# Two attention layers and two ReLU layers on one core: the beginning in another order, and exponentials split only while work is overdue

## The chip, the core and the metric

The kernel runs on one NeuronCore of a Trainium2 chip. Its engines work side by side, each through its own queue of instructions: TensorE (PE in the profile, its weight loads PEld), VectorE (DVE), ScalarE (ACT), GpSimd (POOL), and SyncE (SP), which here issues all DMAs. The metric is the device time of one execution in microseconds (us); the median over several runs counts, and lower is better. For this kernel about 0.5% (11 us) is what a measurement can tell from no change.

## The reference

Four layers follow one another on x of 2048 rows by 512 columns, all in float32, each with a layer norm in front and a residual sum behind it; the weights are the same in both rounds.

```python
def _A_ref(x, wq, wk, wv, wo):            # H = 32 heads, Dh = 16, one shared key and value head
    q = (x @ wq).reshape(B, S, H, Dh).transpose(0, 2, 1, 3)
    k = x @ wk
    v = x @ wv
    scores = jnp.einsum("bhqd,bkd->bhqk", q, k) * (Dh ** -0.5)
    p = _softmax(scores, axis=-1)
    o = jnp.einsum("bhqk,bkd->bhqd", p, v)
    return o.transpose(0, 2, 1, 3).reshape(B, S, H * Dh) @ wo

def _B_ref(x, w1, w2):                    # 512 -> 1792 -> 512
    h = jnp.maximum(jnp.einsum("bsd,df->bsf", x, w1), 0)
    return jnp.einsum("bsf,fd->bsd", h, w2)

x = x + _A_ref(_layernorm(x), wq, wk, wv, wo)
x = x + _B_ref(_layernorm(x), w1, w2)
x = x + _A_ref(_layernorm(x), wq, wk, wv, wo)
x = x + _B_ref(_layernorm(x), w1, w2)
```

## The kernel before

**Units, steps, products.** A unit `U` is four heads for a block of 512 queries; there are 32 units in each of the two rounds. Its keys are taken in 16 tiles of 128. One (unit, key tile) pair is a *step*; there are 1024. A step has two score halves (`scores`: eight small matmuls from `fqop` and `fkop` into a PSUM bank `fst`, then one exponential of 128x1024 on ScalarE into `fp`) and one *product* (`values`: 16 small float32 matmuls of `fp` with the values `fva`, summed in the two banks `facc`). The first 16 steps are units 0 to 3 with the first four key tiles each, the next 16 go back through units 3 to 0 with the next four, and so on. When a unit's stretch ends, `keep` empties the two banks on VectorE (or one of them on ScalarE) into `faccs`; the next unit's products wait for that. Four `fp` buffers let the scores run up to four steps ahead of the products.

**Split exponentials.** In `cut_values` an exponential's float32 bits are taken apart: the upper 16 bits are read as bfloat16, and VectorE writes the rest as float16 over the lower 16 bits (`cut`, two subtractions of 128x1024). The product then takes 24 small 16-bit matmuls instead of 16 in float32. A step so treated is called a cut below. Values for it lie in `fvp`, high and low part, which `keep_keys` fills from `fva`.

**Dense work.** Projections, output and ReLU layers are Python generators in `self.gens`; each `yield 1.0` is one unit of TensorE work. The whole program is laid out in straight order when it is built. `timed` decides at each point whether the next thing on TensorE is a score half, a product or a unit of dense work, by an account of its own (`_Account`, `duration`) that adds up durations for each engine, and a beam search over the next 24 moves. Each step adds `rate` (at least 1) to `due`, the work owed; work may be placed once `due` is at least 1 (`LEAST`), and what stands above 11 (`OVER`) is penalised. A cut is decided when the first exponential of a step ends:

```python
            if chance and self.now >= chance[0][0] - LATE:
                e1, e, i = chance.pop()
                if (self.asked and self.gens and not pend and i > j and self.coming > NEAR
                        and self.sim.at["DVE"] <= max(self.now, e1) + LATE):
                    self.cuts.add(i)
```

`self.asked` counts the chains (output, ReLU layer, next projections) that have been started, so there is no cut before the first of them. `HALF` is the time that half a cut is thought to take on VectorE. Functions can also be hung on a product with `at(i, fn)`; `after(i)` calls them once product `i` has been placed, behind the `keep` of a unit that ends there.

**The beginning (`begin`).** Four row tiles of x are loaded, then the key, value and query weights. VectorE makes their layer norm (`stats`, two small operations on GpSimd in between, `apply` to `fxn`), TensorE transposes them in turn (`transposed`), ScalarE copies the high half and VectorE subtracts the low half, into `fxt`. Behind each, six warm matmuls (`warm`, into `facc`) keep TensorE busy. Weights are split in the same way: `prep_wkv` (wk2 high and low), `prep_wq` for query group 0, later 1, later 2 and 3. `late_consts` fills `va[0]` and `vp[0]` on GpSimd and makes further constants. Then come the key block (`key_rows`, `keep_keys`, `key_norm`: the largest key square is turned, reduced to a row `fkr` and sent into the key operand), and the first query group (`first_query`), whose high half goes to the scratch `fqd` in DRAM in two DMAs and whose low half goes in one. `squares` sums the query squares; for groups 0 and 1 its rows `fqr` go straight into the query operands `fqop`. `load_rows` brings units 0 and 1 back from `fqd` in four DMAs. After that group 1 is formed and projected, 16 warm matmuls follow, and the last two query groups are formed. Only then does `timed` take over with the generator `following` in hand: the squares and loads for units 2 and 3, `rows(8)` (row tiles 4 to 7: `stats`, `apply`, `halved` into `fxp`, a transposing DMA each), then the keys of blocks 1 to 3. Tiles 8 to 15 hang on products 1, 3, 7 and 9.

SP's queue is taken in order: a DMA that waits holds back those behind it.

Of the kernel before, what the change touches and what calls it, by code (L numbers as in the profile page):

```python
# [37 lines left out]
LATE, NEAR, HALF = 0.3, 8, 1.22  # L38
# [20 lines left out]
class _Account:  # L59

    def __init__(self, clear=0.0):
        self.at = {"ACT": 0.0, "DVE": 0.0, "POOL": 0.0, "SP": 0.0, "PE": 0.0}
        self.slots, self.turns, self.uses = {}, {}, {}
        self.form, self.boxes = None, {}
# [62 lines left out]
    def run(self, eng, out, ins, cost):  # L127
        start = max(self.at[eng], self.after(eng, ins, False), self.after(eng, [out], True))
        end = self.at[eng] = start + cost
        if eng == "SP":  # L130
            end += LAND + cost_of(out) * SIZE[out.dtype] * count(out) / FLOW
            eng = "DMA"
# [21 lines left out]
def duration(eng, op, out, ins):  # L154
# [12 lines left out]
    if eng == "DVE":  # L167
        if psum or len([a for a in ins if cost_of(a) > 1]) > 1 or op == "bn_stats":
            return 0.15 + n / 960.0
# [10 lines left out]
class _Engine:  # L180
# [4 lines left out]
    def __getattr__(self, op):  # L185
        fn = getattr(self.eng, op)

        def call(*a, **k):
# [3 lines left out]
            if op == "dma_start":  # L192
                self.account.run("SP", out, ins, TURNED if k.get("transpose") else ISSUE)
# [16 lines left out]
class _Engines:  # L210

    def __init__(self, nc, account):
# [4 lines left out]
        self.sync = _Engine(account, nc.sync, "SP")  # L217


class _Net:  # L220
# [185 lines left out]
    def late_consts(self):  # L406
        nc = self.nc
        nc.gpsimd.memset(self.va[0], self.vs / self.os)
        if not self.exact:
            nc.gpsimd.memset(self.vp[0], self.vs / self.os)  # L410
            nc.gpsimd.memset(self.wms, 0.0)
            wv = self.wt("wvc", [P, 4, DH], bufs=1)
            nc.gpsimd.tensor_copy(wv, self.wvraw[:, :, 1, :])
            self.spread(wv.rearrange("p c d -> p (c d)"), 3, 0)
            nc.gpsimd.memset(self.good, 1.0)
            nc.vector.memset(self.sel, 0.0)
            grp = self.ct("grp", [P, 2, 4])
            nc.vector.reduce_sum(grp.rearrange("p s g -> p (s g)"),
                                 self.ident.rearrange("p (g d) -> p g d", d=DH), axis=AX)
            nc.vector.tensor_add(self.sel[:, 0:4], grp[:, 0], grp[:, 1])  # L420
# [8 lines left out]
    def prep_wkv(self, raw, eng=None):  # L429
# [16 lines left out]
        nc.gpsimd.tensor_sub(self.wk2[1], rr, _f(self.wk2[0]))  # L446
        self.wvraw = raw

# [7 lines left out]
    def prep_wq(self, raw, lo=0, hi=4, tmp=None):  # L456

        nc = self.nc
        if tmp is None:
            tmp = self.wt("p", [P, 4, D], bufs=self.np)  # L460
        if hi - lo < 4:
            for g in range(lo, hi):
                t, r = tmp[:, :, g * P:(g + 1) * P], raw[:, :, g * P:(g + 1) * P]
                for pr in range(2):
                    nc.scalar.activation(t.rearrange("p c (q x d) -> p c q x d", q=2, x=4)[:, :, pr],
                                         r.rearrange("p c (x q d) -> p c x q d", x=4, q=2)[:, :, :, pr],
                                         AF.Copy, scale=self.up / self.xs * DH ** -0.5)
            cols = slice(lo * P, hi * P)
            nc.scalar.activation(self.wq2[0][:, :, cols], tmp[:, :, cols], AF.Copy)
            (nc.gpsimd if lo > 1 else nc.vector).tensor_sub(self.wq2[1][:, :, cols], tmp[:, :, cols], self.wq2[0][:, :, cols])  # L470
            return tmp
# [123 lines left out]
    def keep_keys(self, L, b, pv):  # L595
        nc = self.nc
        nc.vector.tensor_copy(self.va[L][:, 4 * b:4 * b + 4, 0:DH], pv[:, :, 48:64])
        if not self.exact:
# [4 lines left out]
            v, vp = self.va[L][:, 4 * b:4 * b + 4, 0:DH], self.vp[L][:, 4 * b:4 * b + 4]  # L603
            nc.vector.tensor_copy(vp[:, :, 0:DH], v)
            nc.vector.tensor_sub(vp[:, :, 32:48], v, vp[:, :, 0:DH])
        if self.exact or b + 1 != self.normed[L]:
            self.have[L] += 1

# [29 lines left out]
    def squares(self, L, b, groups, sq):  # L638
# [10 lines left out]
        qr = self.wt("qr", [P, 2, D], F16, bufs=1)  # L649
        for pr in range(2):  # L650
            rows = slice(0, 32 * n)
# [1206 lines left out]
```

## Time and profile before

| | |
|---|---|
| median of 3 runs | 2245.5 us (2242.57 to 2253.92) |
| the profiled execution | 2249.38 us, span 2247.6 us |
| TensorE busy | 2162.8 us, 96% |
| ScalarE busy | 1980.6 us, 88%; 1949.1 us of it 2048 exponentials |
| VectorE busy | 1231.6 us, 55%; 505.8 us of it 376 halves of split exponentials |
| GpSimd busy | 279.3 us, 12% |
| first exponential | starts at 32.53 us |

Nearly all instructions pass through one helper, so their line is L189 throughout, and they are told apart by the tiles they write and read (with an `f` in front: `fst<-fqop,fkop` are scores). A row of the timeline has the start, the duration, the engine, and behind it in brackets how long the engine had idled and who ended that. Rows of merged instructions have their count behind an x.

### The profile page before, as it was taken

Reading aid. Unit: us, or ns where it says so; the run is one execution under the profiler, and the core shown is the slowest. Engines: PE = TensorE matmul, PEld = TensorE weight load, DVE = VectorE, ACT = ScalarE, POOL = GpSimd, SP = SyncE. Lnnn points to the kernel's source line nnn. Section 1 sums busy time; section 2 is a strip of 40 time slices with the busy share of each in tenths; the row PEclk is TensorE's granted clock in tenths of the full one; section 3 lists DMA queues with packets and bytes.
Section 4 is the critical chain, followed back from the end, with each engine's and each line's share of the span. In section 5 each row is a group of like instructions: output and inputs, shape, how many; then the busy total and the mean of one; then the engine's idle time right before and its main releaser. Section 6 shows DMA issues by size and latency. Waiting matters only on the chain.

```text
span 2247.6 us, 127404 instructions
## 1 busy us (share of the span) xinstructions
PE 2162.8 (96%) x59949; PEld 1266.5 (56%) x59949; DVE 1231.6 (55%) x1961; ACT 1980.6 (88%) x2111; POOL 279.3 (12%) x321
## 2 busy tenths in 40 slices
PE   7999999999999999999999999999999999999988
PEld 3444445556667864665546555456656655665543
DVE  7426635554565555544676676565634554654642
ACT  5899999999989999999988889889999999999810
POOL 6216830001100021000120021100010000100000
PEclk8999999999999999999999999999999999999999
DMA  5235634111332133221252154532124211312122
GB/s 156 72 109 173 200 103 109 59 49 48 84 104 68 46 95 92 69 68 39 82 130 71 38 141 141 142 87 68 40 73 118 68 49 64 100 42 73 52 81 71
DMA packets 182561, 195.08 MB, mean 87 GB/s; under 512 B 79312, under 2 KB 115712, under 8 KB 181768
## 3 DMA queue, kind: packets, MB, share of 16 engines
q1 hardware_dynamic: 182024, 186.83, 28.1%
q8 instruction: 470, 7.70, 1.4%
q14 instruction: 67, 0.55, 0.1%
HBM read 120.16 MB, written 51.87 MB: 77 GB/s over the span
## 4 chain that ended last, share of the span: by engine, by line
PE 78%; ACT 11%; DVE 5%; issue 2%; DMA 2%; POOL 1%; SPq 0%; DVEq 0%; ACTq 0%; POOLq 0%
PE fmisc L189 31%; PE facc L189 31%; PE fst L189 16%; ACT fp L189 11%; DVE fbst L189 1%; DMA frd<-flsum 1%; DMA fqop<-fqd 1%; DVE faccs L189 0%; DVE fxt L189 0%; SPq L189 0%; DVE fxn L189 0%; DVE fp L189 0%; DVE fqr L189 0%; DMA frinv<-frd 0%; POOL fbmv L189 0%
## 5 line engine op out<-in xcount | busy, mean ns | idle before, releaser
L189 ACT ACTIVATE fp<-fst 128x1024 f32<-128x1024 f32 x2048 | 1949.1, 1030 | 140.2 <-PE fst L189 128.4
L189 PE MATMUL fst<-fqop,fkop 64*32 64x512 f16 x16384 | 952.2, 378 | 43.2 <-ACT fp L189 36.5
L189 PE MATMUL facc<-fp,fva 64*32 64x512 f32 x13376 | 937.8, 593 | 3.3 <-issue 2.0
L189 DVE TENSOR_TENSOR fp<-fp 128x1024 f16<-128x1024 f32 x376 | 505.8, 1398 | 257.5 <-ACT fp L189 257.0
L189 PEld LDWEIGHTS <-fkop 64*32 64x32 f16 x16384 | 382.8, 91 | 460.5 <-issue 347.1
L189 PEld LDWEIGHTS facc<-fp,fva 64*32 64x32 f32 x13376 | 296.9, 106 | 100.2 <-issue 26.4
L189 PE MATMUL fmisc<-fw,fhh 64*32 64x512 f16 (+1 forms) x6384 | 314.3, 377 | 5.1 <-DVE fseen L189 3.1
L189 PEld LDWEIGHTS <-fw 64*32 64x32 f16 (+1 forms) x9576 | 201.6, 93 | 132.5 <-issue 41.8
L189 PE MATMUL fmisc<-fxt,fw 64*32 64x512 f16 (+1 forms) x5544 | 241.1, 376 | 2.1 <-DVE fxt L189 0.9
L189 POOL TENSOR_SCALAR fbmv<-fbmv 128x1 f32<-128x1 f32 x64 | 18.0, 281 | 1560.9 <-DVE fbmv L189 1559.8
L189 PE MATMUL fmisc<-fw,fhl 64*32 64x512 f16 (+1 forms) x3192 | 202.3, 378 | 0.0
L189 PEld LDWEIGHTS <-fhh 64*32 64x32 f16 (+1 forms) x6384 | 142.9, 93 | 87.7 <-issue 39.3
L189 PE MATMUL facc<-fp,fvp 64*32 64x512 f16 (+2 forms) x4512 | 178.2, 386 | 1.7 <-issue 1.7
L189 DVE SCALAR_TENSOR_TENSOR fxt<-fmisc,fxt 128x512 f32<-128x512 f32 x156 | 102.6, 684 | 126.2 <-PE fmisc L189 125.9
L189 PE MATMUL fmisc<-fxq,fw 64*32 64x512 f16 x4032 | 150.1, 376 | 3.3 <-issue 3.1
L189 DVE TENSOR_SCALAR fhh<-fmisc 128x512 f16<-128x512 f32 x98 | 67.2, 686 | 124.5 <-PE fmisc L189 124.4
L189 DVE COPY fseen<-fmisc 1x1 f32<-1x1 f32 x266 | 29.1, 141 | 193.1 <-PE fmisc L189 187.8
L189 DVE TENSOR_TENSOR faccs<-faccs,facc 128x512 f32<-128x512 f32 x116 | 79.6, 686 | 66.6 <-PE facc L189 51.8
L189 PEld LDWEIGHTS <-fvp 64*32 64x32 f16 (+1 forms) x4512 | 89.7, 90 | 44.6 <-issue 10.9
L189 PE MATMUL fmisc<-fwo,fot 64*32 64x512 f16 x2688 | 103.8, 378 | 2.3 <-issue 2.2
L189 DVE SCALAR_TENSOR_TENSOR fhl<-fmisc,fhh 128x512 f16<-128x512 f32 x112 | 77.5, 692 | 28.4 <-ACT fhh L189 25.0
L189 PEld LDWEIGHTS <-fhl 64*32 64x32 f16 (+1 forms) x3192 | 72.8, 93 | 28.6 <-issue 3.0
(139 smaller groups left out, 1114.4 us busy)
## 6 DMA issues: line engine op xcount, KB each, us to landing
fw<-fwd SPq DMA_DIRECT2D x224, 256.0 KB
fod<-faccs SPq DMA_DIRECT2D x62, 256.0 KB
fqop<-fqd SPq DMA_DIRECT2D x152, 98.0 KB
fxt<-in_A_x_dram SPq DMA_DIRECT2D x32, 256.0 KB
fqd<-fqh SPq DMA_DIRECT2D x64, 128.0 KB
foraw<-fod SPq DMA_DIRECT2D x31, 256.0 KB
frinv<-frd SPq DMA_DIRECT2D x31, 256.0 KB
faccs<-in_B_w_dram SPq DMA_DIRECT2D x28, 256.0 KB
```

The source lines that it names most:

```text
L189: r = fn(*a, **k)
```

## The change

Six things are changed.

- `begin`: `va[0]` and `vp[0]` are filled by ScalarE (`filled`, two activations) before the first weights are there, not by GpSimd later. The low half of the key weights is subtracted behind the last row tile: GpSimd first copies one element of it. Query group 0 is scaled and formed on ScalarE behind the second row tile, the second group and the scaling of the others behind the last. The low halves of the two groups are subtracted on VectorE around the other constants (`consts`).
- The two query groups are projected one behind the other. The key copy's transposes stand after the fifth product of the first, the key maximum after its last; the squares and the loads of units 0 and 1 stand after the ninth product of the second, which has a PSUM bank of its own. Twelve warm matmuls follow instead of 16.
- In `squares` the first group's second half is scaled by ScalarE, and the rows go out in four DMAs instead of two.
- `value_halves` of the first block, the statistics of row tiles 4 to 7 and the forming of the last two groups come after both queries. Row tiles 8 to 11 are loaded before the queries instead of behind them.
- In `following`, `rows(6)` stands ahead of the loads of units 2 and 3; tiles 8 to 15 hang on products 5, 7, 11 and 13.
- The planner: `due >= 3.0` is asked of every cut, `HALF` is 1.4, and VectorE operations over 1000 wide (of the kinds named) are put 0.18 higher. `ACTQ` keeps an account for DMAs of ScalarE's queue; none are issued there.

```diff
-LATE, NEAR, HALF = 0.3, 8, 1.22
+LATE, NEAR, HALF = 0.3, 8, 1.4
...
-            return 0.15 + n / 960.0
+            return (0.33 if n > 1000 else 0.15) + n / 960.0
...
+    def filled(self):
+        for t in (self.va[0], self.vp[0]):
+            flat = t.rearrange("p k c -> p (k c)")
+            self.nc.scalar.activation(flat, self.nhalf.to_broadcast([P, flat.shape[1]]), AF.Copy,
+                                      scale=-2.0 * self.vs / self.os)
...
+        low = lambda: nc.gpsimd.tensor_sub(self.wk2[1], rr, _f(self.wk2[0]))
+        return low if eng else low()
...
+    def formed_wq(self, tmp, lo, hi):
+        cols = slice(lo * P, hi * P)
+        self.nc.scalar.activation(self.wq2[0][:, :, cols], tmp[:, :, cols], AF.Copy)
+        eng = self.nc.gpsimd if lo > 1 else self.nc.vector
+        return lambda: eng.tensor_sub(self.wq2[1][:, :, cols], tmp[:, :, cols], self.wq2[0][:, :, cols])
...
-            v, vp = self.va[L][:, 4 * b:4 * b + 4, 0:DH], self.vp[L][:, 4 * b:4 * b + 4]
-            nc.vector.tensor_copy(vp[:, :, 0:DH], v)
-            nc.vector.tensor_sub(vp[:, :, 32:48], v, vp[:, :, 0:DH])
+            if L or b:
+                self.value_halves(L, b)
...
+            if early and pr and not groups[0]:
+                nc.scalar.activation(qr[rows, pr], ps[pr][rows], AF.Copy, scale=2 * SLACK / ONE)
+                continue
             nc.vector.tensor_scalar(qr[rows, pr], ps[pr][rows], 2 * SLACK / ONE, None, op0=MUL)
...
                 for u in range(2):
-                    dst = self.qop[2 * G + u].rearrange("(h r) p q -> h r p q", r=64)[:, 48]
-                    nc.sync.dma_start(dst, qr[2 * u:2 * u + 2])
+                    for h in range(2):
+                        nc.sync.dma_start(
+                            self.qop[2 * G + u][64 * h + 48:64 * h + 49], qr[2 * u + h:2 * u + h + 1])
...
         self.high(qh, ps)
         send((0, qh), (2, qh))
-        between(1)
-        nc.vector.tensor_sub(ql, ps, qh)
+        between(12)
         sq[G] = self.wt("sq", [P, D], BF16, bufs=4)
         nc.gpsimd.tensor_mul(sq[G], qh, qh)
+        nc.vector.tensor_sub(ql, ps, qh)
         send((1, ql))
...
         self.zero_rows(self.qop[0:2])
+        self.filled()
         self.warm(20)
...
             yield from self.transposed(xn[t], t, self.xt2)
+            if t == 1:
+                self.scaled_wq(qraw, tmp, 0, 1)
+                lows = [self.formed_wq(tmp, 0, 1)]
+            if t == 2:
+                nc.gpsimd.tensor_copy(self.wt("seen", [1, 1]), xn[3][0:1, 0:1])
+                low()
             self.warm(6)
+        self.scaled_wq(qraw, tmp, 1, 2)
+        lows.append(self.formed_wq(tmp, 1, 2))
+        self.scaled_wq(qraw, tmp, 2, 4)
         for t in range(4, 8):
             self.load_x(t)
         self.fixed_rows(self.qop[0:2])
-        tmp = self.prep_wq(qraw, 0, 1)
-        self.late_consts()
+        lows[0]()
+        self.consts()
+        lows[1]()
+        for t in range(8, 12):
+            self.load_x(t)
         self.zero_rows(self.qop[2:4])
         self.fixed_rows(self.qop[2:4])
         kv = yield from self.key_rows(0, 0, self.xt2)
...
-        yield from self.squares(0, 0, [0], sq)
-        for U in range(2):
-            self.load_rows(U, self.qop[U], 0, 48)
-        self.prep_wq(qraw, 1, 2, tmp)
-        yield from self.first_query(1, sq, lambda k: None)
-        for t in range(8, 12):
-            self.load_x(t)
+        def squared(k):
+            if k == 8:
+                for _ in self.squares(0, 0, [0], sq):
+                    pass
+                for U in range(2):
+                    self.load_rows(U, self.qop[U], 0, 48)
+
+        bank = self.pp.tile([P, D], F32, name=self.tag + "acc2", bufs=1)
+        yield from self.first_query(1, sq, bank, squared)
+        self.formed_wq(tmp, 2, 4)()
+        for r in range(4, 8):
+            self.pre[r] = self.stats(self.xin[r])
+        self.value_halves(0, 0)
         self.sq, self.sent = sq, 2
-        self.warm(16)
-        self.prep_wq(qraw, 2, 4, tmp)
+        self.warm(12)
...
         yield from self.squares(0, 0, [1], sq)
+        self.rows(6)
         for U in range(2, 4):
             self.load_rows(U, self.qop[U], 0, 48)
...
-                if (self.asked and self.gens and not pend and i > j and self.coming > NEAR
+                if (self.asked and self.gens and due >= 3.0 and not pend and i > j and self.coming > NEAR
...
-            for i, t in ((1, 10), (3, 12), (7, 14), (9, 16)):
+            for i, t in ((5, 10), (7, 12), (11, 14), (13, 16)):
                 at(i, self.rows, t)
```

90 lines of the change are left out of this document (47 added, 43 removed).

## The prediction

> **What bounds the kernel now.** I read the page first (share of each engine, the costliest groups), then the waits of the long middle, then the beginning by timeline and by windows of 2 us.
>
> ```profile
> span 2247.6 us, 127404 instructions
> PE 2162.8 (96%) x59949; PEld 1266.5 (56%) x59949; DVE 1231.6 (55%) x1961; ACT 1980.6 (88%) x2111; POOL 279.3 (12%) x321
> ...
> L189 DVE TENSOR_TENSOR fp<-fp 128x1024 f16<-128x1024 f32 x376 | 505.8, 1398 | 257.5 <-ACT fp L189 257.0
> ```
>
> TensorE is the bound over the whole, but not in every stage. The 376 subtractions on VectorE are the halves of 188 split exponentials ("cuts"). Waits of TensorE, and of ScalarE, between 350 and 2100 us (total us, times, longest):
>
> ```profile
> PE fst L189 <- ACT fp L189: 18.8, 41, 1.2
> ```
>
> ```profile
> ACT fp L189 <- PE fst L189: 112.9, 181, 3.1
> ```
>
> There ScalarE waits for TensorE, and TensorE for ScalarE only 18.8 us. By windows of 50 us (PE, PEld, DVE, ACT, POOL busy):
>
> ```profile
> 50.00:100.00 50.00, 47.87 (x1094) 24.29 (x1089) 23.37 (x50) 42.11 (x45) 16.62 (x18) 0.90 0.42 102
> 150.00:200.00 50.00, 46.60 (x1191) 23.47 (x1175) 20.77 (x45) 49.74 (x54) 16.34 (x13) 1.00 0.56 172
> ```
>
> From 100 to about 350 us ScalarE is full (49.74 of 50) and TensorE is not; later TensorE is full. Nothing in either stage gives time back, so what is saved before 100 us should reach the end one for one.
>
> **The change part by part.** The beginning first, from the timeline (start, duration):
>
> ```profile
> 6.16 0.90 ACT L189 ACTIVATE foraw<-faccs 128x192 f32<-128x192 f32 x4 [4.16 <-DMA faccs<-in_A_wk_dram]
> ...
> 7.80 1.15 POOL L189 TENSOR_TENSOR fwkl<-foraw,fwkh 128x512 f16<-128x512 f32 x1
> 8.10 1.14 DVE L189 TENSOR_SCALAR fxn<-fxt,fbmv 128x512 f32<-128x512 f32 x1
> ...
> 10.57 0.52 DVE L189 TENSOR_SCALAR fxn<-fxt,fbmv 128x512 f32<-128x512 f32 x1
> ...
> 11.81 1.53 DVE L189 TENSOR_SCALAR fxn<-fxt,fbmv 128x512 f32<-128x512 f32 x1
> ...
> 18.03 0.60 ACT L189 ACTIVATE fkv<-fmisc 128x512 f32<-128x512 f32 x1 [2.08 <-PE fmisc L189]
> ...
> 21.52 0.18 DVE L189 CAST fvp<-fva 128x64 f16<-128x64 f32 x1
> ...
> 21.74 0.23 DVE L189 TENSOR_TENSOR fvp<-fva,fvp 128x64 f16<-128x64 f32 x1
> ...
> 23.24 1.28 SPq L189 DMA_DIRECT2D fkop<-fkr  x2
> ...
> 24.61 0.62 SPq L189 DMA_DIRECT2D fqd<-fql  x1
> ...
> 25.33 1.08 SPq L189 DMA_DIRECT2D fqop<-fqr  x2
> ...
> 27.26 1.76 SPq L189 DMA_DIRECT2D fqop<-fqd  x4
> ...
> 29.52 1.91 PE L189 MATMUL facc<-fident 128*128 128x256 f16 x16
> ...
> 30.21 1.32 ACT L189 ACTIVATE fp<-fp 128x256 f32<-128x256 f32 x4
> ...
> 31.36 0.63 PE L189 MATMUL fst<-fqop,fkop 64*32 64x512 f16 x16
> ...
> 31.57 1.06 ACT L189 ACTIVATE fwqh<-fp 128x1024 f16<-128x1024 f32 x1
> ```
>
> Fills. The same scaling of a row tile takes 0.52 us alone, 1.14 us beside GpSimd's subtraction at 7.80, and 1.53 us at 11.81, when GpSimd makes the fills. The fills of `va` and `vp` go to ScalarE and the key weight's low half (fwkl) is put behind the last row tile, so 0.6 and 1.0 us leave VectorE's chain. The transposes and their slow clock then take over as the limit; I give the key copy 0.7 us (between 0.4 and 1.6). The fills cost ScalarE at most 2 x 1.06 us (the 1024-wide copy at 31.57) in the 4.16 us that it idles before the first weights land. The scaling of the other three query groups and the forming of the second now stand ahead of the key copy on ScalarE: six times 0.33 (1.32 / 4) and at most 1.06, 3.0 us from about 14 us on, just inside the copy's new place near 17.3; if the weights land later, the term shrinks by as much.
>
> First query. Deferring `value_halves` takes 0.18 + 0.23 = 0.4 us out of VectorE's way to the key maximum. So `ql` comes 1.1 us earlier; its store, behind the two key-row DMAs on SP, goes from 24.61 to 23.5. The row loads now start 2.65 us after that store (27.26 - 24.61), so they could start at 26.15. But the query-square rows go out in four DMAs instead of two, ahead of the loads on SP: at 0.54 each 2.16 us from about 24.55, to 26.7; at half the price the store decides again. I take 26.5, that is 0.75 earlier. The second query's stores are now queued behind these loads, and units 2 and 3 wait for them; they are not needed before step 8, some 15 us on. The loads of x tiles 8 to 11 are now ahead of the fixed rows of queries 2 and 3 on SP, needed equally late. GpSimd's short wait for the last row tile holds back only the low key half and the constants, used after 15 us.
>
> What the loads meet, from windows of 2 us (PE, PEld, DVE, ACT, POOL; then granted clock, DMA share, GB/s):
>
> ```profile
> 24.00:26.00 2.00, 1.17 (x5) 0.40 (x5) 1.60 (x3) 0.00 (x0) 0.00 (x0) 0.99 0.22 71
> 26.00:28.00 2.00, 2.00 (x7) 0.64 (x5) 0.00 (x0) 0.00 (x0) 0.00 (x0) 0.50 0.22 62
> 28.00:30.00 2.00, 2.00 (x10) 1.01 (x9) 0.00 (x0) 0.28 (x1) 0.00 (x0) 0.66 0.63 177
> 30.00:32.00 2.00, 2.00 (x32) 1.37 (x30) 0.69 (x1) 1.97 (x6) 1.04 (x1) 1.00 0.15 35
> ```
>
> The loads' traffic is over by some 30.4 us, unit 0's by about 29.5, but TensorE has the second query (from 24.5 to 29.5, most of it at half clock) and 16 warm products before the scores, and ScalarE forms the weights' second half (31.57 to 32.6) before the first exponential. The change runs the second query straight behind the first, at full clock: 12 products, the two squares and 12 warm ones end near 25.9. Scores then wait for the rows, at 29.5 - 0.75 = 28.75, and the first exponential starts near 29.4 instead of 32.53: 3.1 us. Against it stands a gap of 2.9 us on TensorE in front of the scores. In the rows above, a half-busy 24 to 26 was followed by a clock of 0.50. A step needs 2 x 0.22 + 0.86 = 1.30 us of TensorE (rows below) and 1.85 of ScalarE (9.24 / 10 x 2); at half clock 2.6, so a stretch of 3.4 us (the granted clock is low from about 26.0 to 29.4 above) would lose about 0.95. I take 0.7, and 2.4 us for the term, between 1.0 and 3.1. The Trainium skill (TensorE: Matmul & The Clock Gate, HAM oscillation) puts the limit at idle gaps over about 3.4 us; by it 2.9 us is harmless and the sum would be 0.7 us better. The row is stricter here: the clock fell although TensorE had been busy 1.17 of 2 us.
>
> Row tiles. ScalarE between 32 and 110 us, then what stood before it:
>
> ```profile
> ACT fp L189 <- PE fst L189: 9.8, 10, 2.7
> ```
>
> ```profile
> 32.53 9.24 ACT L189 ACTIVATE fp<-fst 128x1024 f32<-128x1024 f32 x10
> ...
> 50.47 1.03 ACT L189 ACTIVATE fp<-fst 128x1024 f32<-128x1024 f32 x1 [2.71 <-PE fst L189]
> 52.54 1.02 ACT L189 ACTIVATE fp<-fst 128x1024 f32<-128x1024 f32 x1 [1.05 <-PE fst L189]
> 54.12 9.50 ACT L189 ACTIVATE fp<-fst 128x1024 f32<-128x1024 f32 x10 [0.56 <-PE fst L189]
> ...
> 70.97 1.02 ACT L189 ACTIVATE fp<-fst 128x1024 f32<-128x1024 f32 x1 [2.35 <-PE fst L189]
> ```
>
> ```profile
> 47.23 0.68 DVE L189 TENSOR_TENSOR faccs<-faccs,facc 128x512 f32<-128x512 f32 x1
> ...
> 47.96 0.22 PEld L189 LDWEIGHTS facc<-fp,fva 64*32 64x32 f32 x14 [1.66 <-DVE faccs L189]
> ```
>
> The first hole (2.71 + 1.05 + 0.56 = 4.3 us): the sum of unit 0 is emptied only at 47.23, behind the row tiles on VectorE's queue; TensorE stalls, and its clock falls. The change takes the statistics of four tiles into the idle wait for the loads, and moves the later tiles from products 1, 3, 7, 9 to 5, 7, 11, 13: unit 0 ends at product 3 before tiles 8 and 9 are queued, units 1 and 2 at products 7 and 11 ahead of the tiles put there. I take 4.0 us back, between 1.0 and 4.3. The rest of the 9.8 is 5.5 us, 2.35 of it in front of step 16, which waits for the second key block. That block's tiles come as early as now, but its emptying (some 3.4 us of VectorE) can fall behind tiles 12 and 13. I take 1.5 us, between a loss of 1.5 and a gain of 3.5.
>
> Cuts. A plain product and a cut one, in the middle:
>
> ```profile
> 1200.06 0.48 PE L189 MATMUL fst<-fqop,fkop 64*32 64x512 f16 x8
> 1200.28 1.12 PE L189 MATMUL facc<-fp,fva 64*32 64x512 f32 x16
> 1201.14 0.48 PE L189 MATMUL fst<-fqop,fkop 64*32 64x512 f16 x8
> ...
> 1202.22 0.96 PE L189 MATMUL facc<-fp,fvp 64*32 64x512 bf16 x24
> 1202.90 0.50 PE L189 MATMUL fst<-fqop,fkop 64*32 64x512 f16 x8
> ```
>
> From start to start 0.86 against 0.68: a cut saves TensorE 0.18 us and costs VectorE 2 x 1.398. Every cut not taken where TensorE is the bound costs 0.18 us; the slack of 18.8 us would hide some 100 of them. Dense work is due at one unit or more a step and is pressed only above 11 (OVER), so where TensorE is behind, due stands far above the new 3.0 and cuts go on; where it falls below 3, a missed cut only lets due rise to 3. The planner's half goes from 1.22 to 1.40, and its other VectorE costs over 1000 wide by 0.18: nearer to the 1398 measured, and with VectorE thought busier, some chances fail (they need it free within 0.3 us). I put it at about 10 cuts lost where they count, +1.7 us; between -2 (fewer misplaced products) and +10 (55 lost there).
>
> Sum: -2.4 - 4.0 - 1.5 + 1.7 = -6.2. The profiled execution took 2249.4 us (span 2247.6); 2243.2 would follow. It lies 3.9 above the median 2245.5 (2242.6 to 2253.9), so I forecast 2239 for a median.
>
> **The rivals.** (1) Everything at the beginning comes through: 3.1 and all 9.8 us of holes, 12.9: 2232.6. For it: each hole has a VectorE queue or the clock behind it, and both are touched. Against: the second key block is still on the same queue.
> (2) The wait moves. TensorE idles from 25.9 until the rows land; with the clock at 0.50 the scores start slow, and step 16 waits for its keys as now: 1.0 + 1.0 + 0 back, 2243.5. The falling clock after 24 to 26 and the 2.35 us speak for it; against it, ScalarE needs TensorE only 1.30 of 1.85 us. The Trainium skill's clock gate (same page and section) would make it so from 3.4 us of idleness on.
> (3) Slower: the threshold of 3.0 takes cuts away where TensorE is the bound. 46 of 188 such cuts use up the 8 us of the beginning (46 x 0.18 = 8.3); at 65 the time is 2245.5 - 7.9 + 11.7 = 2249; over 105 it is slower by 0.5%. For it: TensorE waits for ScalarE in only 41 places, so few cuts are free. Against it: due must stay under 3 for so long while the work is behind.
>
> **How the numbers follow.** Half a percent (11.2 us) is about what a measurement of this kernel tells from no change. Forecast 0.53; rival 1 0.22, rival 2 0.13, rival 3 0.12, half of it beyond 2256.7. So faster by over 0.5% (under 2234.3) 0.24, within it 0.70, slower 0.06. The range for 8 in 10 goes from a little under rival 1, 2229, to rival 3's 2249; the forecast's own is 2234 to 2244.
>
> **What would show it.** The first exponential near 29 to 31 us instead of 32.53; the second query's products at 0.22 us apart and a gap on TensorE behind them; row-tile scalings all near 0.52 before 12 us; the emptying of unit 0 within 3 us of its last product and no hole of over 1 us before step 15; step 16 near 63 us instead of 70.97; 330 to 375 subtractions of 128x1024. It is wrong if far fewer of these show up with more TensorE time in the middle, or if a hole as wide as the old ones opens in front of step 16.

## The result, and the profile after

The changed kernel took 2229.42 us (median of 8 runs, 2221.73 to 2235.44) against 2242.1 us before (8 runs, 2238.9 to 2253.92). The ratio of the two is 0.9931, with a 95% interval of 0.9914 to 0.9947: 15.5 us faster, between 11.9 and 19.3 (the interval reaches 4 us to either side, less than the 11 us that I had named as what a measurement can tell from no change). I had forecast 2239 us, and gave "faster by over 0.5%" a chance of 0.24. In what follows, a gain in us is a kernel's ratio less one, times the median of the kernel before as measured beside it; negative is faster.

The profiled execution after took 2224.62 us, 24.8 less than the profiled one before (2249.38). The latter lies 7.3 above its median of 8 and the former 4.8 below its own, so the two traces show more than the change is worth. The page of the kernel after, its first two lines and two groups of part 5 (idle ahead of the group, and its releasers, at the end):

```profile
span 2222.7 us, 127244 instructions
PE 2147.8 (97%) x59873; PEld 1255.0 (56%) x59873; DVE 1207.4 (54%) x1944; ACT 1980.6 (89%) x2112; POOL 280.3 (13%) x320
...
L193 ACT ACTIVATE fp<-fst 128x1024 f32<-128x1024 f32 x2048 | 1948.6, 1031 | 124.3 <-PE fst L193 110.4
...
L193 DVE TENSOR_TENSOR fp<-fp 128x1024 f16<-128x1024 f32 x358 | 481.5, 1397 | 255.5 <-ACT fp L193 255.4
```

The exponentials are as long as before (the same group before stands in the next fence), but ScalarE idles 15.9 us less ahead of them (124.3 against 140.2). There are 358 subtractions where there were 376: nine cuts fewer.

```profile
L189 ACT ACTIVATE fp<-fst 128x1024 f32<-128x1024 f32 x2048 | 1949.1, 1030 | 140.2 <-PE fst L189 128.4
```

To see where the time went I matched the 2048 exponentials of two traces by number, two to a step, and took the difference of their starts. That is a reading of one profile of each kernel:

| start of step | after - before | e1 (new beginning alone) | e2 (planner's edits alone) |
|---|---|---|---|
| 0 | -1.08 | -0.25 | -0.26 |
| 4 | +0.53 | +2.14 | -0.26 |
| 12 | -4.30 | -2.69 | -2.11 |
| 16 | -6.65 | -5.05 | -3.19 |
| 24 | -9.45 | -7.85 | -4.69 |
| 128 | -11.19 | -9.22 | -5.10 |
| 576 | -9.18 | -5.54 | -6.50 |
| 704 | -15.46 | -8.89 | -12.98 |
| 832 | -20.03 | -8.76 | -17.19 |
| 1023 | -22.93 | -9.07 | -19.27 |

Two stretches give time: the beginning up to step 24, and steps 576 to 1023, far from any line of the beginning. Windows of 300 us show the second (PE, PEld, DVE, ACT, POOL busy with counts; then granted clock, DMA share, GB/s), before and then after:

```profile
1200.00:1500.00 300.00, 287.62 (x8392) 159.03 (x8379) 197.65 (x296) 262.11 (x275) 28.77 (x35) 0.99 0.39 111
1500.00:1800.00 300.00, 296.46 (x8879) 190.73 (x8871) 151.36 (x229) 281.67 (x299) 8.17 (x12) 1.00 0.24 72
```

```profile
1200.00:1500.00 300.00, 290.72 (x8500) 186.92 (x8490) 185.37 (x292) 268.51 (x281) 28.83 (x35) 1.00 0.38 111
1500.00:1800.00 300.00, 298.04 (x9003) 177.99 (x8994) 162.75 (x234) 288.65 (x308) 8.21 (x12) 1.00 0.23 70
```

In the same 600 us TensorE is busy 4.7 us longer (588.76 against 584.08) and issues 232 more matmuls, and ScalarE makes 15 more activations (589 against 574). So the middle goes faster because more of the time is filled. The waits between 350 and 2100 us say it too, first those of TensorE, then those of ScalarE, after:

```profile
PE fst L193 <- ACT fp L193: 17.9, 43, 1.2
```

```profile
ACT fp L193 <- PE fst L193: 101.2, 167, 3.1
```

TensorE's wait for ScalarE has hardly changed (18.8 before), ScalarE's for TensorE fell from 112.9 us in 181 places to 101.2 in 167.

The beginning after, ScalarE's timeline (start, duration, in brackets the idle before):

```profile
31.45 5.61 ACT L193 ACTIVATE fp<-fst 128x1024 f32<-128x1024 f32 x6 [5.34 <-PE fst L193]
38.15 1.03 ACT L193 ACTIVATE fp<-fst 128x1024 f32<-128x1024 f32 x1 [1.10 <-POOL fbmv L193]
39.38 12.11 ACT L193 ACTIVATE fp<-fst 128x1024 f32<-128x1024 f32 x13 [0.20 <-PE fst L193]
51.65 9.52 ACT L193 ACTIVATE fp<-fst 128x1024 f32<-128x1024 f32 x10 [0.15 <-PE fst L193]
62.38 46.58 ACT L193 ACTIVATE fp<-fst 128x1024 f32<-128x1024 f32 x48 [1.22 <-PE fst L193]
```

The holes of 2.71 and 2.35 us of the kernel before are gone; the widest left is 1.22 us, in front of step 15. But the first exponential starts at 31.45, not near 29.4. SP's queue, TensorE, and windows of 2 us of the same trace tell why:

```profile
23.69 0.62 SPq L193 DMA_DIRECT2D fqd<-fql  x1
24.55 2.42 SPq L193 DMA_DIRECT2D fqop<-fxp  x4
27.07 1.94 SPq L193 DMA_DIRECT2D fqop<-fqd  x4
```

```profile
24.36 1.47 PE L193 MATMUL facc<-fident 128*128 128x256 f16 x12
...
29.70 0.62 PE L193 MATMUL fst<-fqop,fkop 64*32 64x512 f16 x4 [3.86 <-DMA fqop<-fqd]
...
30.78 1.04 PE L193 MATMUL fst<-fqop,fkop 64*32 64x512 f16 x12 [0.47 <-DMA fqop<-fqd]
```

```profile
26.00:28.00 2.00, 0.00 (x0) 0.09 (x1) 1.93 (x5) 0.11 (x1) 2.00 (x2) 1.00 0.03 4
28.00:30.00 2.00, 0.30 (x4) 0.10 (x3) 1.32 (x6) 0.00 (x0) 1.67 (x5) 0.52 0.65 178
30.00:32.00 2.00, 1.53 (x18) 0.35 (x15) 0.09 (x1) 0.56 (x1) 1.67 (x5) 0.50 0.46 134
32.00:34.00 2.00, 1.41 (x17) 0.24 (x16) 2.00 (x4) 2.00 (x3) 0.01 (x1) 0.50 0.26 86
...
36.00:38.00 2.00, 2.00 (x32) 0.78 (x24) 1.97 (x6) 1.05 (x2) 1.83 (x3) 0.50 0.48 91
```

The four one-row DMAs of the query squares hold SP 2.42 us, so the row loads start at 27.07, only 0.19 earlier than before (27.26). TensorE is empty for 3.86 us, and from 28.1 to 38.3 (the trace's record of the clock) it runs at 0.50, 10.2 us.

### The profile page after: what moved, and what is told of

Its sections match the earlier page's. It is cut to its first block, busy times and chain, and to the rows that moved or that the text cites. A ratio compares the mean times of both kernels' runs of the same rounds, so it can differ in the third digit from the quotient of the medians.

```text
span 2222.7 us, 127244 instructions
## 1 busy us (share of the span) xinstructions
PE 2147.8 (97%) x59873; PEld 1255.0 (56%) x59873; DVE 1207.4 (54%) x1944; ACT 1980.6 (89%) x2112; POOL 280.3 (13%) x320
## 4 chain that ended last, share of the span: by engine, by line
PE 77%; ACT 17%; DVE 3%; issue 2%; DMA 1%; POOL 1%; SPq 0%; ACTq 0%; DVEq 0%; POOLq 0%
PE fmisc L193 30%; PE facc L193 30%; ACT fp L193 16%; PE fst L193 16%; DVE fxt L193 0%; DVE fbst L193 0%; DVE faccs L193 0%; DVE fp L193 0%; DVE fkop L193 0%; DMA fw<-fwd 0%; POOL fxp L193 0%; POOL fbmv L193 0%; DVE fkv L193 0%; DMA fxr<-fxt 0%; DVE fxn L193 0%
## 5 line engine op out<-in xcount | busy, mean ns | idle before, releaser
L193 ACT ACTIVATE fp<-fst 128x1024 f32<-128x1024 f32 x2048 | 1948.6, 1031 | 124.3 <-PE fst L193 110.4
L193 PE MATMUL fst<-fqop,fkop 64*32 64x512 f16 x16384 | 936.2, 378 | 45.4 <-ACT fp L193 36.2
L193 DVE TENSOR_TENSOR fp<-fp 128x1024 f16<-128x1024 f32 x358 | 481.5, 1397 | 255.5 <-ACT fp L193 255.4
L193 PEld LDWEIGHTS <-fw 64*32 64x32 f16 (+1 forms) x9576 | 208.9, 93 | 119.9 <-issue 35.4
L193 PE MATMUL fmisc<-fxt,fw 64*32 64x512 f16 (+1 forms) x5544 | 236.0, 376 | 3.1 <-issue 1.6
L193 POOL TENSOR_SCALAR fbmv<-fbmv 128x1 f32<-128x1 f32 x64 | 18.8, 294 | 1555.0 <-DVE fbmv L193 1554.1
L193 PE MATMUL fmisc<-fw,fhl 64*32 64x512 f16 (+1 forms) x3192 | 196.5, 378 | 0.0
L193 PEld LDWEIGHTS <-fhh 64*32 64x32 f16 (+1 forms) x6384 | 135.7, 93 | 93.4 <-issue 42.4
L193 PE MATMUL facc<-fp,fvp 64*16 64x512 bf16 (+2 forms) x4296 | 167.2, 386 | 0.0
L193 PEld LDWEIGHTS <-fvp 64*32 64x32 f16 (+1 forms) x4296 | 84.4, 90 | 41.0 <-issue 10.9
L193 PEld LDWEIGHTS <-fhl 64*32 64x32 f16 (+1 forms) x3192 | 68.2, 93 | 32.6 <-issue 4.6
```

Of the source, the lines that this page charges most:

```text
L193: r = fn(*a, **k)
```

## The experiments

Two theories stood against the prediction (C in what was expected) at first: that the beginning is worth more than forecast and the planner's edits about nothing (B), and that the beginning is worth roughly what was forecast and the planner's edits are a gain (A). Later a third came in (E): what the planner's edits change is the arrangement of the dense work, and any disturbance of its numbers draws a new arrangement, a better or a worse one. Its counterpart (D) says that the edits act by being better numbers.

### The two halves of the change

e1 has the new beginning, and the planner as it was:

```diff
-LATE, NEAR, HALF = 0.3, 8, 1.4
+LATE, NEAR, HALF = 0.3, 8, 1.22
-            return (0.33 if n > 1000 else 0.15) + n / 960.0
+            return 0.15 + n / 960.0
-                if (self.asked and self.gens and due >= 3.0 and not pend and i > j and self.coming > NEAR
+                if (self.asked and self.gens and not pend and i > j and self.coming > NEAR
```

> The new beginning with the planner's old numbers (HALF 1.22, old VectorE cost, no due >= 3.0). Theory A (the beginning gives about 10 us, the planner's edits the rest): 9 to 11 us faster than before, behind the full change by 2 to 5. Theory B (all of it is the beginning, and the later gain in the one trace is scatter between executions): as fast as the full change, 12 to 15 us. Theory C (my prediction: planner costs 1.7 us): a little faster than the full change, 14 to 17 us. In the trace the exponential of step 56 comes 10 us earlier than before in each.

e2 is the reverse: the old beginning, and these three edits as the change has them. 

> The old beginning with all of the planner's edits. Theory A: 2 to 5 us faster than before, all of it behind step 128. Theory B: within 1.5 us of before. Theory C: 1 to 3 us slower.

e3 is the kernel before with the threshold `due >= 3.0` alone. 

> Before with only due >= 3.0 asked of a cut. If missed cuts cost TensorE (prediction): fewer cuts, 0.18 us slower for each one lost, 0 to 3 us in all. If they are lost only where TensorE has slack: 5 to 15 cuts fewer and the same time within 1.5 us. If the cuts held VectorE up for other work: 2 to 5 us faster.

e4 is the kernel before with the two prices alone (HALF 1.4, and 0.33 over 1000 wide). 

> Before with only HALF 1.4 and the higher VectorE cost. Theory A with the durations as its cause: 2 to 5 us faster, with less TensorE idle time behind step 128. Theory B: within 1.5 us. Theory C: 1 to 3 us slower by lost chances.

Measured: e1 0.9968 (0.9952 to 0.9983), -7.2 us. e2 0.9951 (0.9932 to 0.9971), -11.0. e3 0.9987 (0.9972 to 1.0002), -2.9. e4 1.0013 (0.9996 to 1.003), +2.9. The beginning is worth about the 7.9 us that I had forecast for it, and theory B falls. C falls with e2, which gains. A is right in kind but not in size: it had e1 at 9 to 11 us and e2 at 2 to 5, and e2 lies between 6.5 and 15.3 us faster. The planner's edits gain with the old beginning too, but not as a sum of parts: threshold and prices alone come to nothing together, and to 11 us when both are in. The groups of e1's and of e2's exponentials and of e2's subtractions:

```profile
L193 ACT ACTIVATE fp<-fst 128x1024 f32<-128x1024 f32 x2048 | 1950.8, 1030 | 136.5 <-PE fst L193 122.6
```

```profile
L189 ACT ACTIVATE fp<-fst 128x1024 f32<-128x1024 f32 x2048 | 1949.8, 1031 | 121.3 <-PE fst L189 107.0
...
L189 DVE TENSOR_TENSOR fp<-fp 128x1024 f16<-128x1024 f32 x362 | 487.1, 1398 | 252.3 <-ACT fp L189 252.1
```

With the planner's edits ScalarE's idle falls from 140.2 to 121.3 us, with the new beginning alone only to 136.5. Cuts do not follow the time: e1 has 352 halves, e2 362, e3 364, e4 346. For steps 576 to 1023, summed from the traces:

| | us | TensorE idle | at low clock | halves |
|---|---|---|---|---|
| before | 920.7 | 19.6 | 3.4 | 190 |
| e1 | 917.1 | 16.3 | 3.4 | 176 |
| e2 | 907.9 | 15.7 | 0 | 183 |
| after | 906.9 | 12.3 | 0 | 181 |

From e1 to after 10.2 us go, with 5 halves more: 4.0 us of it is TensorE's idle time, and 3.4 us of half clock, worth at most 1.7 us, is gone. The rest is TensorE's time while it works, which the totals don't take apart further.

### Around the planner's numbers

Four kernels step one number of the changed kernel. e5: `due >= 2.0`. 

> The full change with due >= 2.0 instead of 3.0. Theory D (the planner's edits act through their meaning: VectorE rightly priced, no cut without need): within 2 us of the full change, 11 to 17 us faster than before. Theory E (any edit of the planner's numbers draws another layout of the middle, and this draw is a lucky one): some 3 to 8 us of the later gain is gone, 5 to 10 us faster than before. In either, the exponential of step 56 stays where the full change has it.

e6: `due >= 4.0`. 

> The full change with due >= 4.0. As for 2.0: theory D within 2 us of the full change; theory E somewhere between 5 and 15 us faster than before, not the same as with 2.0.

e7: HALF 1.35 and 0.30 in place of 1.4 and 0.33. 

> The full change with HALF 1.35 and 0.30 instead of 1.4 and 0.33, still near the 1.398 us measured. Theory D: within 2 us of the full change. Theory E: a draw of its own, 5 to 15 us faster than before.

Measured: e5 0.9942 (0.9922 to 0.9963), 350 halves; e6 0.9963 (0.9947 to 0.998), 336 halves; e7 0.9934 (0.9917 to 0.9951), 354 halves. Theory D wanted all three within 2 us of the change's 15.5: e7 is, e5 is just outside, e6 is 7 us away. In e6 lost cuts go with a loss: its steps 576 to 1023 hold 159 halves against 181, and take 918.4 us against 906.9 with 18.2 us of idle TensorE. That would be rival 3 of the prediction, at 4.0 and not yet at 3.0; but e13 below comes out at the same time with 360 halves, and e9, with 342, is at least as fast as the change, so it isn't shown that the lost cuts are the cause.

e9 and e10 take the two kinds of edit apart on the new beginning. e9 has the prices without the threshold:

```diff
-                if (self.asked and self.gens and due >= 3.0 and not pend and i > j and self.coming > NEAR
+                if (self.asked and self.gens and not pend and i > j and self.coming > NEAR
```

> The full change without due >= 3.0: new beginning, HALF and the VectorE cost only. If the threshold and the prices work only as a pair (old beginning: each alone nothing, both 11 us): no better than the new beginning alone, 4 to 10 us faster than before. If the new beginning makes one of them work alone: 11 to 16 us.

e10 has the threshold without the prices. 

> The full change with the old HALF and VectorE cost: new beginning and due >= 3.0 only. As a pair: 4 to 10 us faster than before; otherwise 11 to 16 us.

Measured: e9 0.9917 (0.9904 to 0.9931), -18.6 us; e10 0.995 (0.9932 to 0.9968), -11.2. So the threshold named in the change's title is not needed for the gain: without it the kernel is at least as fast as with it (0.9931). e9's subtractions:

```profile
L193 DVE TENSOR_TENSOR fp<-fp 128x1024 f16<-128x1024 f32 x342 | 459.6, 1396 | 256.1 <-ACT fp L193 255.9
```

It makes 17 cuts fewer than the kernel before, and is at least as fast as the one after. At the 0.18 us that I charged they would cost 3.1 us. Nothing of that is to be seen, but it is less than what the arrangement can move (below), so no kernel here shows what a lost cut costs.

The third theory was tried with four kernels on the new beginning. e13 has HALF 1.4 alone. 

> The new beginning with HALF 1.4 alone (old VectorE cost, no threshold). If the planner's price of a half cut is the cause: 14 to 19 us faster than before, as with both prices. If the account of VectorE is: 5 to 10 us, as the beginning alone.

e14 has the 0.33 alone. 

> The new beginning with the VectorE cost 0.33 alone. If the account of VectorE is the cause: 14 to 19 us faster than before; if HALF is: 5 to 10 us.

e15 and e16 keep the planner as before and disturb it in a number that has nothing to do with cuts, the time it books for an exponential or for a copy:

```diff
-SCORE, VALUE, DENSE, EXP = 0.216, 0.858, 0.2155, 0.925
+SCORE, VALUE, DENSE, EXP = 0.216, 0.858, 0.2155, 0.93
```

> The new beginning with the old numbers of the planner but one nudge that corrects nothing: the exponential thought to take 0.930 us instead of 0.925. If a layout gains only by right prices: within 2.5 us of the beginning alone (7 us faster than before). If each nudge draws a layout of its own and the draws lie several us apart: anything from 2 to 15 us faster, and not the same as the other nudge.

```diff
-TO_ACT, TO_PE, COPY = 0.2, 0.2, 1.8
+TO_ACT, TO_PE, COPY = 0.2, 0.2, 1.9
```

> The new beginning with the old numbers and the other nudge: the emptying of a unit thought to take 1.9 us instead of 1.8. As for the first nudge: within 2.5 us of the beginning alone, or a draw of its own between 2 and 15 us faster than before.

Measured: e13 0.9963 (0.9948 to 0.9978), -8.3; e14 0.9945 (0.9929 to 0.9961), -12.4; e15 0.9984 (0.997 to 0.9998), -3.6; e16 0.9949 (0.993 to 0.9968), -11.5. HALF alone does no more than the beginning alone; the 0.33 alone comes out between the two ranges. The two disturbances differ from each other by 7.9 us, and their intervals do not meet, though only just: around e1's -7.2 the arrangement alone moves the time by some 4 us to either side, without any better number in it.

All kernels with the new beginning, its SP queue and its 12 warm products, by whether both prices are in: with them -15.5 (after), -13.0 (e5), -8.3 (e6), -14.8 (e7), -18.6 (e9); without -7.2 (e1), -11.2 (e10), -8.3 (e13), -12.4 (e14), -3.6 (e15), -11.5 (e16). The means are -14.0 and -9.0. That the prices themselves are worth some 5 us is suggested by this; with a scatter of 4 us for each arrangement it isn't settled, and e4, the prices alone on the old beginning, speaks against it.

### Inside the beginning

Up to beyond 200 us, nine of the kernels with the new beginning (after, e1, e5, e6, e7, e9, e10, e13, e14) issue the same instructions in the same order on TensorE, ScalarE and VectorE (but for single matmul records that stand one place apart or are missing), and so do four with the old one (before, e2, e3, e4). So their traces are nine and four executions of one beginning each. Starts of exponentials against the profile of before, mean and range:

| start of step | old beginning (4) | new beginning (9) | difference of means |
|---|---|---|---|
| 0 | +0.1 (-0.3 to +0.8) | -1.2 (-1.95 to -0.25) | -1.2 |
| 4 | +0.1 (-0.3 to +0.8) | +0.8 (-0.6 to +2.1) | +0.7 |
| 12 | -0.8 (-2.1 to +1.0) | -4.1 (-5.4 to -2.7) | -3.3 |
| 24 | -2.7 (-4.7 to 0.0) | -9.2 (-10.5 to -7.85) | -6.5 |
| 128 | -3.0 (-5.1 to 0.0) | -10.9 (-12.5 to -9.2) | -7.9 |

The profile of before is the latest of the four at steps 24 and 128: its clock was low at 46.4 to 53.2 and 66.9 to 73.7 us, e3's only at 45.9 to 49.3. The nine stand 2.7 us apart at step 4 and still 2.7 at step 24: from the one to the other each gains between 9.95 and 9.99 us on the profile of before. So what is won or lost ahead of step 4 goes through one for one, and changes behind it are best counted from there.

e8 puts the later row tiles back to where they stood:

```diff
-            for i, t in ((5, 10), (7, 12), (11, 14), (13, 16)):
+            for i, t in ((1, 10), (3, 12), (7, 14), (9, 16)):
```

> The full change with the later row tiles back on products 1, 3, 7 and 9. If the new places close the first hole (prediction: 4.0 us, and 1.5 in front of step 16), step 24 comes 4 to 6 us later than in the full change, with a hole of 2 us or more before step 12, and the run is 4 to 6 us slower. If the early statistics alone close it, step 24 is within 1.5 us.

Measured: 0.9952 (0.9937 to 0.9967), which does not part from the changed kernel's 0.9931. Its trace does. ScalarE's timeline, in front of steps 7 and 14:

```profile
46.38 1.02 ACT L193 ACTIVATE fp<-fst 128x1024 f32<-128x1024 f32 x1 [1.06 <-PE fst L193]
...
63.34 47.50 ACT L193 ACTIVATE fp<-fst 128x1024 f32<-128x1024 f32 x50 [2.01 <-PE fst L193]
```

Holes come back, smaller than before and a step or two earlier (2.01 us in front of step 14, where the changed kernel has 1.22 in front of step 15). Its step 24 stands at -7.02 and its step 128 at -7.48, later than in any of the nine kernels of the table, whose means are -9.2 and -10.9. Counted from step 4, where e8 stands at -0.55, it gains 6.5 us up to step 24 and 6.9 up to step 128, where the nine gain 10.0 and 11.7. So by this one execution, whose clock also fell once more (43.6 to 47.0), the row tiles' new places are worth 3.5 us at step 24 and 4.7 at step 128, about the 4 to 6 expected; the rest of the gain at the holes comes from what stands ahead of them.

e12 sends the query-square rows in two DMAs again:

```diff
-                    for h in range(2):
-                        nc.sync.dma_start(
-                            self.qop[2 * G + u][64 * h + 48:64 * h + 49], qr[2 * u + h:2 * u + h + 1])
+                    dst = self.qop[2 * G + u].rearrange("(h r) p q -> h r p q", r=64)[:, 48]
+                    nc.sync.dma_start(dst, qr[2 * u:2 * u + 2])
```

> The full change with the query-square rows in two DMAs as before. Prediction's bound: the four took 2.42 us of SP, two took 1.08, so the loads start when the low half has landed, 0.7 us earlier (26.3 instead of 27.07), and the first exponential with them; 0.5 to 1 us faster, which only the trace can show. If the loads are held by something else: no change at 27.07.

SP's queue, TensorE and ScalarE in e12:

```profile
24.41 1.09 SPq L193 DMA_DIRECT2D fqop<-fxp  x2
26.38 1.76 SPq L193 DMA_DIRECT2D fqop<-fqd  x4
```

```profile
28.55 1.32 PE L193 MATMUL fst<-fqop,fkop 64*32 64x512 f16 x16 [2.85 <-DMA fqop<-fqd]
```

```profile
29.49 5.60 ACT L193 ACTIVATE fp<-fst 128x1024 f32<-128x1024 f32 x6 [3.53 <-PE fst L193]
```

Two DMAs of two rows take 1.09 us of SP, four of one row 2.42: the price is by the DMA, not by the row. The loads start at 26.38 and the first exponential at 29.49, 1.95 earlier than in the changed kernel, where about 0.7 was expected. Only 0.69 of it is the earlier start of the loads (26.38 against 27.07). From there to the first exponential 3.11 us pass, against 4.38: the first scores come 2.17 us behind the loads' start and not 2.63, all 16 matmuls in one run, where the changed kernel waits 0.47 us more for another load behind the first four. Why the rows come sooner behind two DMAs than behind four stays open. At step 24 e12 stands at -11.50, earlier than any of the nine. The whole kernel, 0.9928 (0.9914 to 0.9942), can't show the 2 us.

e11 fills TensorE's gap with 44 warm products for 12, `self.warm(44)`. 

> The full change with 44 warm products in front of the scores instead of 12, 32 x 0.11 = 3.5 us more, so that TensorE has no gap there. If the gap halves the clock (0.50 from 28 to 38 us in the trace of the full change) and that costs: no low clock between 28 and 40, step 4 is 2 to 3 us earlier, step 24 the same lead or less, 1 to 3 us faster than the full change. If the exponentials take up the slack: step 24 unchanged.

Measured: 0.9935 (0.9918 to 0.9951). TensorE, then ScalarE, in e11:

```profile
24.07 4.97 PE L193 MATMUL facc<-fident 128*128 128x256 f16 x44
...
29.32 0.40 PE L193 MATMUL fst<-fqop,fkop 64*32 64x512 f16 x4 [0.28 <-DMA fqop<-fqd]
...
30.65 0.61 PE L193 MATMUL fst<-fqop,fkop 64*32 64x512 f16 x12 [0.94 <-DMA fqd<-fqh]
```

```profile
31.10 3.77 ACT L193 ACTIVATE fp<-fst 128x1024 f32<-128x1024 f32 x4 [5.29 <-PE fst L193]
35.80 14.86 ACT L193 ACTIVATE fp<-fst 128x1024 f32<-128x1024 f32 x16 [0.93 <-PE fst L193]
```

The gap falls from 3.86 to 0.28 us, but the low clock, which I had expected to be gone, only shrinks from 10.2 to 3.4 us (32.0 to 35.5). Step 4 comes 0.9 us earlier than in the changed kernel, not 2 to 3; at step 24 e11 stands at -11.04, 1.6 us ahead of it. By step 1023 it is 8.0 behind it (-14.95 against -22.93): the warm products change what the planner reckons with, and from the first stage on e11's instructions stand in another order.

### The best of both

e17 and e18 join what had looked best: the prices without the threshold (e9), the query-square rows in two DMAs (e12); e17 with 36 warm products, e18 with 12. 

> The new beginning with both prices, no threshold, the query-square rows in two DMAs and 36 warm products instead of 12. If the parts add up: first exponential near 29.5 us with no low clock behind it, step 24 some 12 us ahead of before, 17 to 21 us faster than before. If the beginning's change draws another layout of the middle: 10 to 16 us.

> The same with 12 warm products as in the full change: first exponential near 29.5 us, a low clock of 7 to 10 us behind it, step 24 some 11 us ahead of before, 16 to 20 us faster; if the layout of the middle is drawn anew, 10 to 16 us.

Measured: e17 0.9959 (0.9943 to 0.9975), 2237.52 us. e18 0.9901 (0.9884 to 0.9919), 2226.37 us (2220.17 to 2228.93) beside 2247.56 before: 22 us faster, and the best of the kernels here, and more than the 16 to 20 expected; its interval and that of the changed kernel (0.9914 to 0.9947) just overlap. ScalarE's timelines, e17 and then e18:

```profile
29.69 17.61 ACT L193 ACTIVATE fp<-fst 128x1024 f32<-128x1024 f32 x19 [3.43 <-PE fmisc L193]
```

```profile
29.55 5.61 ACT L193 ACTIVATE fp<-fst 128x1024 f32<-128x1024 f32 x6 [3.40 <-PE fst L193]
...
61.13 46.58 ACT L193 ACTIVATE fp<-fst 128x1024 f32<-128x1024 f32 x48 [1.22 <-PE fst L193]
```

e17 has the best beginning of all: no low clock from 5.9 to 565.7 us, 19 exponentials without a hole, step 24 at -13.84 (e18: -10.70). And it is the slower of the two by 0.6%, because the middle gave nothing: step 1023 at -16.0 against -23.2. With -9.2 us it misses both of its ranges. But for the two DMAs, e18 issues the instructions of e9 in the same order to the end, as e12 does those of the changed kernel. So two arrangements were measured twice, -18.6 and -22.2, -15.5 and -16.2, and kept their rank; 36 warm products draw another one. A gain of 3 us at the beginning is less than what another arrangement can cost.

## Why the prediction was right or wrong

The step that failed is the planner's term, which was wrong in sign. The sum for the beginning came out right, but its parts did not, and that it held is luck.

**First exponential** (-2.4 us, 1.0 to 3.1): it came 1.08 us earlier (1.2 by the means), and at step 4, behind the slow clock that I had charged to this term, the kernel was 0.53 us behind (0.7 by the means). So the term gave nothing. Three of its sizes were off. I had the four DMAs end at 26.7, or the store decide, and took 26.5; they took 2.42 us and the loads started at 27.07. From there to the first exponential I had 2.9 us (26.5 to 29.4), and it took 4.38 (31.45 less 27.07). And the gap on TensorE was 3.86 us and not 2.9, and the clock was low for 10.2 us and not 3.4: between steps 0 and 4 the nine kernels lose 1.2 to 2.5 us on the profile of before, whose clock is full there, and I had charged 0.7. With two DMAs (e12) the loads go at 26.38 and the first exponential stands at 29.49, beside the 29.4 of the working. The row-tile scalings came out as said, all at 0.51 to 0.54 us:

```profile
8.10 0.52 DVE L193 TENSOR_SCALAR fxn<-fxt,fbmv 128x512 f32<-128x512 f32 x1
...
11.83 0.54 DVE L193 TENSOR_SCALAR fxn<-fxt,fbmv 128x512 f32<-128x512 f32 x1
```

**First hole** (-4.0, 1.0 to 4.3): counted from step 4, behind the slow clock, to step 12 the means gained 3.9 us. This part was right. The queue did what was said: unit 0 is emptied at 42.63, not at 47.23.

```profile
41.83 0.69 DVE L193 COPY faccs<-facc 128x512 f32<-128x512 f32 x1 [3.52 <-PE facc L193]
42.63 0.69 DVE L193 TENSOR_TENSOR faccs<-faccs,facc 128x512 f32<-128x512 f32 x1
```

I had said that no hole of over 1 us would stand before step 15. One of 1.10 us does, in front of step 3. Its row (38.15) names GpSimd's `fbmv` as what ended it, but an exponential does not use that tile, and the operations on it end at 37.23 and 38.34. What it follows are its own scores, which end at 38.03: TensorE starts them at 37.36, behind a product that takes 1.95 us at the low clock, and 1.05 at the full one:

```profile
35.65 1.95 PE L193 MATMUL facc<-fp,fva 64*32 64x512 f32 x16
37.36 0.67 PE L193 MATMUL fst<-fqop,fkop 64*32 64x512 f16 x8
...
39.45 1.05 PE L193 MATMUL facc<-fp,fva 64*32 64x512 f32 x16
```

In e17, whose clock stayed full, there is no such hole.

**Step 16** (-1.5, from 1.5 lost to 3.5 gained): it starts at 64.32 instead of 70.97, near the 63 that I named, and between steps 12 and 24 the means gained 3.2 us, twice what I had taken; a further 1.4 came up to step 128, for which I had no term.

Together that is 7.9 us at step 128, by the means, and 7.2 (3.8 to 10.8) by e1's time, against the 7.9 of my three terms. The 3 us that the first term lacked were made up by 3 us of later gains that I had not sized. Rival 2, the wait that moves, is out as a time, though its slow scores came. Rival 1 counted all 9.8 us of holes; some 3 us of them (the means of the old beginning at steps 24 and 128) were that one execution's.

**Cuts** (+1.7, -2 to +10): the step that failed. The number of cuts was right (9 cuts lost, about 10 forecast). But I priced the planner's edits by the cuts alone, at 0.18 us each, and took the low end, -2, as "fewer misplaced products". They were worth -8.3 us on the new beginning (-15.5 less -7.2; the two intervals, 11.9 to 19.3 and 3.8 to 10.8 faster, do not meet) and -11.0 on the old. The row to read was in the prediction, ScalarE waiting 112.9 us for TensorE in 181 places: a change of any number in the planner moves those places, and I had set its two ends by the cuts instead of by that row. The two disturbances show the size that a bound needed: 7.9 us from one to the other. That the threshold is not what gains is shown (e9), and so is that a mere rearrangement can move the time by some 8 us (e15 against e16). Whether the better prices have a share in the gain, and why this arrangement is the better one, stays open.

**The clock.** I had charged 0.7 us for the slow stretch and called the row stricter than the rule of the Trainium skill (TensorE: Matmul & The Clock Gate, HAM oscillation), which sets the limit at idle gaps over about 3.4 us. In the changed kernel the gap grew to 3.86 us, so by both the clock should fall; but it fell at 28.06, only 2.2 us after the last warm product (24.36 + 1.47 = 25.83). e18 tells the two apart. Its TensorE, and its windows:

```profile
28.64 1.07 PE L193 MATMUL fst<-fqop,fkop 64*32 64x512 f16 x16 [2.77 <-DMA fqop<-fqd]
```

```profile
28.00:30.00 2.00, 1.20 (x18) 0.35 (x18) 1.56 (x7) 0.45 (x1) 1.66 (x5) 1.00 0.62 161
30.00:32.00 2.00, 0.87 (x16) 0.23 (x16) 2.00 (x5) 2.00 (x3) 1.75 (x4) 0.72 0.48 150
```

The gap is 2.77 us, the clock is still full after it, and falls at 30.9 in the half-busy stretch that follows, for 6.8 us. So a gap below the rule's limit was not harmless here, and the stricter reading of the row was the right one. The price is larger than I took: between steps 0 and 4 e18 loses 2.2 us against e17, which kept its clock (from -2.98 to -0.71, against -2.84 to -2.81). The 1.0 us more by which e17 leads at step 24 comes behind step 12, with a full clock in both, and e17's instructions stand in another order there.

## What to carry to other kernels

Where a planner lays out the work, a change of its numbers is a new arrangement: its bounds are set by the waits that the arrangement decides, not by the operation that the number is about, and it is worth running two neutral disturbances before a gain is put down to a better number. A stretch of one profile should be held against other executions of the same instructions before its holes are counted as gain; here the one shown made them some 3 us larger than they are. Count DMAs on a queue by the piece, and don't take an idle gap for harmless because it is short.

## What the runs showed of the hardware that I had not expected

- A DMA on SP's queue costs by the piece: four one-row ones 2.42 us, two two-row ones 1.09 (0.60 and 0.55 each).
- The clock fell without a gap of 3.4 us, in e11 after waits of 0.28 and 0.94 us, and stayed full in e17 beside a window as empty. e11's window ahead of the fall at 32.0, then e17's at the same place:

```profile
30.00:32.00 2.00, 0.80 (x14) 0.28 (x15) 0.65 (x2) 0.90 (x1) 1.46 (x4) 1.00 0.48 142
```

```profile
30.00:32.00 2.00, 0.78 (x25) 0.40 (x31) 2.00 (x5) 2.00 (x3) 1.71 (x4) 1.00 0.51 163
```

- Once low, it stayed low for 10.2 us in the changed kernel, though TensorE was busy 1.41 of 2 us or more in each window from 30 to 38 us.
- The same beginning, instruction for instruction, stood up to 4.7 us apart at step 24 with the old order, and 2.7 with the new one. With the new one all of that was there at step 4. With the old one 4.4 came behind step 4, where the clock was low for 13.7 us in before and for 3.4 in e2 and e3.
